# Exchanging real and imaginary spectrum rows with two strided transfers per unit, with a new order of work

## The chip, the cores and the metric

The kernel runs on one core of a Trainium2 chip. The metric is the device time of one execution in microseconds; the profiled span is the same execution from its first to its last instruction, about 2 us less. TensorE is PE, VectorE DVE, ScalarE ACT, GpSimd POOL, SyncE SP; SP issues nearly all transfers.

## The reference, cut to what matters

The result is a sum of three branches over the same normalised input: the input itself, a long convolution per channel, and a gated linear unit (GLU).

```python
xn = _layernorm(x, axis=-1)                       # x: [1, 2048, 512] bf16
# A: K[d,l] = Re sum_n C[d,n] exp(dt A[d,n] l) dB[d,n];  y = irfft(rfft(xn) * rfft(K)) + xn * Dskip
# B: h = sigmoid(xn @ w_gate) * (xn @ w_up);  h @ w_down          # F = 1792
return x + _A_ref(xn, ...) + _B_ref(xn, ...)
```

The convolution is a product of complex spectra. A complex product needs each real part beside the imaginary part of the same frequency, and the other way round. That exchange is what the change is about. The "up-projection" named below is the GLU's `xn @ w_up`.

## The kernel before

PE carries the GLU (672 of its matmuls of 512 columns) and a two-stage Fourier transform by matmul. Of the convolution's work the following parts matter here.

Nearly everything of the convolution lives in one tile of SBUF (the on-chip memory that all engines read), `big`, of 118,112 bytes per partition, cut by hand into regions that are reused: power tables `G` and `H`, input rows `xn`, later the exchange's buffers `xx`, kernel spectra `kb`, products `pp` and so on.

```python
big = const.tile([128, NBIG // 2], BF, name="big")
def at(off, shape, dt=BF):                         # a region of big
    v = big[:, off // 2:(off + n) // 2]
    ...
HOME = dict(xx=[OFF["xn"], OFF["xn"] + US, OFF["xn"] + 2 * US], ...)   # three buffers of 4 KB
```

There are 16 units: 8 pairs of frequency groups, for 2 halves of the channels. For each unit matmuls make the spectrum from a loaded input z, ACT evicts it (copies it out of PSUM, the memory that matmuls write) into `xx[:, 0]`, and transfers write it with real and imaginary rows exchanged into `xx[:, 1]`. A partition block of 64 rows holds 32 real rows and then 32 imaginary ones, so four transfers of 32 rows each do it. DVE then multiplies both copies by the kernel's spectrum, which matmuls make with a loaded constant matrix E. A unit's result v is stored to device memory and loaded again later.

```python
ex = pl.add("ACT", 0.91, fe, [mm], QP, rel=[sl])                       # eviction into xx[:, 0]
sws = [dma("SP", lambda xx=xx, b=b: xx()[32 * b:32 * b + 32, 1, :, :],
           lambda xx=xx, b=b: xx()[32 * (b ^ 1):32 * (b ^ 1) + 32, 0, :, :], deps=[ex], ...)(64 * KB)
       for b in range(4)]
...
pa_ = pl.add("DVE", 1.14, fpa, [ek] + sws, PKD, acq=[psl])             # pp = xx * kb, 128 x 2048
```

The kernel records operations and issues them in a fixed order, the list `ORDER`, found by a search. Each engine runs its instructions in that order. The waits between engines, on counters called semaphores, are not written by hand: they are derived when the program is built, from which instructions touch which bytes of a tile.

Of the kernel before, what the change touches and what calls it, by code (L numbers as in the profile page):

```python
# [59 lines left out]
MAGIC = 12582912.0  # L60
KB = 1024

def _th(s, b, k2):
    return 2 * np.pi * (s * b / 2048.0 + k2 * b / 32.0)

# [23 lines left out]
def _build_M2():  # L89
    M2 = np.zeros((NU, 128, 128))  # L90
    b = np.arange(32)[:, None]
    k2 = np.arange(32)[None, :]
    for g in range(NU):
        for par in range(2):
            s = 2 * g + par
            blk = slice(64 * par, 64 * par + 64)
            M = np.zeros((64, 64))
            if s >= 1:
                t = _th(s, b, k2)
                M[0:32, 0:32] = np.cos(t)  # L100
                M[32:64, 0:32] = np.sin(t)
                M[0:32, 32:64] = -np.sin(t)
                M[32:64, 32:64] = np.cos(t)
            else:
                t0 = 2 * np.pi * k2 * b / 32.0
                M[0:32, 0:16] = np.cos(t0)[:, 0:16]
                M[0:32, 32 + 1:32 + 16] = -np.sin(t0)[:, 1:16]
                M[0:32, 32 + 0] = (-1.0) ** b[:, 0]
                t64 = 2 * np.pi * (32 + 64 * (k2 - 16)) * b / 2048.0
                M[32:64, 16:32] = np.cos(t64)[:, 16:32]  # L110
                M[32:64, 32 + 16:32 + 32] = -np.sin(t64)[:, 16:32]
            M2[g, blk, blk] = M
    return M2

def _build_MAB():
    MA = np.zeros((NU, 128, 128))
    MB = np.zeros((NU, 128, 128))
    k2 = np.arange(32)[:, None]
    b = np.arange(32)[None, :]
    for g in range(NU):  # L120
        for par in range(2):
            s = 2 * g + par
            blk = slice(64 * par, 64 * par + 64)
            A = np.zeros((64, 64))
            B = np.zeros((64, 64))
# [10 lines left out]
            else:  # L136
# [9 lines left out]
                A[32 + 16:64, 32:64] = -2 * np.cos(t64)[16:32]  # L146
                B[16:32, 32:64] = -2 * np.sin(t64)[16:32]
                B[32 + 16:64, 32:64] = -2 * np.sin(t64)[16:32]
            MA[g, blk, blk] = A
            MB[g, blk, blk] = B  # L150
    return MA, MB

def _row(l):
# [22 lines left out]
def _consts():  # L176
# [27 lines left out]
    return dict(SR=f(sr), ident=f(np.eye(128)), S1=f(z1.reshape(128, 2, 128)), S2=f(z2.reshape(128, 2, 128)), M2=f(quads(M2)), SW=f(sw),  # L204
                MAB=f(np.stack([quads(MA, True), quads(MB, True)], axis=2)), E=f(_build_E(M2).reshape(128, NU // 2, 2, NKT, 128).transpose(1, 0, 2, 3, 4)))

UEV = (18, 19, 27, 28, 29, 30, 31, 32, 33, 34, 35, 36, 37, 38, 39, 40, 41, 44, 45, 52)
ON_ACT = (0, 2)
ORDER = [
    1, 0, 4, 37, 38, 28, 47, 39, 27, 40, 41, 2, 3, 48, 49, 5, 50, 12, 29, 51, 17, 52, 53, 42, 23, 24, 26, 10, 44, 30, 31,  # L210
    43, 32, 7, 6, 45, 46, 33, 34, 107, 35, 19, 25, 134, 36, 54, 644, 55, 645, 632, 633, 58, 15, 14, 106, 634, 646, 685, 686,
    131, 11, 59, 695, 121, 696, 675, 680, 105, 108, 109, 94, 93, 676, 8, 22, 9, 92, 681, 132, 655, 638, 639, 656, 95, 96,
    60, 56, 660, 640, 661, 665, 110, 97, 135, 18, 16, 13, 670, 666, 672, 682, 61, 671, 120, 673, 119, 62, 683, 98, 684, 118,
    100, 650, 662, 663, 651, 674, 136, 102, 101, 99, 133, 63, 140, 664, 700, 647, 57, 652, 701, 64, 648, 122, 141, 653, 649,
    123, 654, 20, 690, 691, 180, 146, 692, 693, 657, 66, 103, 104, 142, 694, 667, 658, 65, 67, 668, 659, 669, 227, 68, 147,
    69, 635, 687, 688, 636, 677, 689, 678, 124, 637, 70, 679, 641, 143, 697, 72, 127, 642, 71, 702, 73, 643, 137, 703, 698,
    138, 74, 699, 704, 75, 76, 736, 705, 111, 731, 112, 77, 181, 228, 182, 229, 78, 706, 79, 733, 732, 230, 183, 707, 231,
    81, 139, 148, 80, 114, 734, 82, 708, 738, 735, 155, 83, 737, 128, 739, 232, 184, 84, 185, 740, 186, 85, 713, 87, 187,
    156, 781, 115, 714, 86, 88, 149, 751, 715, 90, 144, 113, 157, 188, 145, 190, 198, 782, 752, 709, 199, 193, 150, 783,
    161, 721, 723, 724, 152, 191, 200, 784, 722, 202, 785, 201, 153, 203, 725, 116, 233, 761, 206, 741, 176, 766, 207, 192,  # L220
    194, 762, 742, 125, 195, 767, 154, 151, 208, 117, 726, 756, 763, 177, 727, 757, 158, 162, 178, 209, 204, 771, 758, 210,
    764, 765, 759, 773, 167, 772, 205, 21, 163, 126, 189, 774, 760, 753, 728, 211, 729, 89, 775, 754, 214, 168, 196, 159,
    212, 129, 169, 730, 213, 160, 755, 215, 743, 746, 170, 164, 216, 744, 747, 91, 217, 218, 745, 171, 197, 219, 165, 234,
    788, 748, 749, 786, 787, 371, 166, 716, 220, 221, 222, 750, 235, 776, 130, 172, 778, 173, 237, 240, 789, 245, 246, 790,
    768, 249, 223, 247, 777, 248, 174, 250, 253, 175, 847, 224, 241, 238, 239, 242, 244, 769, 225, 779, 770, 780, 791, 254,
    839, 792, 793, 255, 256, 432, 433, 257, 251, 817, 258, 259, 226, 402, 840, 260, 261, 794, 263, 403, 236, 717, 799, 372,
    243, 274, 818, 434, 252, 262, 264, 438, 404, 275, 265, 276, 266, 373, 374, 267, 269, 268, 277, 819, 278, 439, 408, 284,
    321, 279, 379, 406, 409, 280, 270, 292, 322, 293, 323, 837, 800, 296, 324, 820, 290, 286, 436, 378, 377, 294, 437, 295,
    297, 271, 801, 272, 287, 300, 273, 375, 298, 821, 291, 440, 289, 285, 405, 435, 301, 441, 838, 325, 407, 454, 376, 302,
    442, 841, 864, 443, 410, 303, 857, 380, 288, 865, 848, 411, 827, 444, 858, 412, 381, 828, 795, 304, 382, 305, 462, 469,  # L230
    802, 807, 867, 455, 445, 868, 463, 413, 306, 456, 464, 808, 308, 803, 283, 383, 307, 281, 447, 814, 812, 414, 384, 310,
    813, 385, 815, 311, 446, 309, 299, 387, 465, 862, 893, 863, 448, 844, 842, 449, 843, 467, 894, 312, 282, 816, 866, 394,
    466, 468, 424, 386, 451, 415, 452, 453, 470, 313, 450, 869, 859, 388, 326, 471, 472, 327, 389, 314, 860, 315, 473, 316,
    872, 331, 395, 339, 332, 392, 390, 416, 393, 391, 317, 417, 457, 873, 870, 396, 333, 861, 458, 340, 474, 822, 475, 341,
    823, 845, 871, 425, 829, 343, 477, 484, 830, 397, 344, 342, 418, 849, 419, 426, 559, 846, 831, 345, 854, 459, 850, 852,
    855, 422, 460, 347, 476, 421, 420, 398, 346, 874, 478, 552, 423, 853, 334, 479, 328, 851, 348, 856, 499, 349, 427, 399,
    834, 336, 337, 835, 875, 482, 876, 481, 483, 480, 428, 485, 900, 809, 486, 400, 553, 832, 350, 461, 554, 833, 810, 429,
    351, 487, 898, 811, 488, 824, 352, 430, 318, 401, 825, 507, 836, 489, 335, 353, 826, 330, 179, 354, 943, 355, 490, 899,
    357, 508, 555, 431, 492, 558, 509, 901, 338, 556, 557, 491, 529, 510, 329, 512, 358, 513, 877, 493, 356, 359, 494, 319,
    511, 360, 910, 361, 495, 497, 496, 320, 902, 362, 911, 363, 945, 364, 365, 953, 878, 498, 366, 622, 620, 618, 369, 367,  # L240
    560, 561, 562, 879, 946, 880, 563, 500, 530, 501, 502, 531, 514, 885, 597, 598, 503, 515, 604, 589, 522, 895, 886, 599,
    896, 897, 624, 504, 603, 516, 517, 505, 564, 903, 601, 602, 600, 565, 605, 523, 506, 524, 887, 518, 582, 519, 566, 616,
    606, 528, 526, 527, 525, 954, 904, 607, 520, 583, 908, 944, 909, 584, 608, 537, 925, 933, 913, 544, 574, 538, 934, 588,
    586, 609, 585, 532, 888, 539, 610, 926, 533, 923, 567, 914, 590, 545, 920, 587, 924, 591, 521, 542, 611, 630, 955, 927,
    568, 540, 543, 541, 918, 546, 569, 592, 956, 921, 919, 593, 626, 922, 534, 535, 594, 912, 957, 547, 905, 573, 595, 570,
    571, 548, 572, 575, 536, 906, 576, 577, 938, 940, 948, 549, 578, 596, 579, 939, 949, 941, 889, 370, 881, 942, 550, 958,
    915, 916, 580, 959, 612, 928, 917, 368, 551, 930, 581, 931, 929, 935, 628, 963, 950, 951, 613, 936, 627, 629, 617, 947,
    907, 932, 960, 937, 952, 614, 961, 619, 962, 964, 890, 623, 615, 891, 967, 965, 710, 625, 892, 711, 966, 631, 712, 621,
    968, 969, 804, 718, 805, 971, 719, 806, 970, 972, 882, 883, 796, 975, 720, 797, 884, 798, 973, 976, 978, 974, 979, 977,
    980, 981]  # L250

class _Op:
    __slots__ = ("alt", "tab", "eng", "cost", "fn", "prio", "acq", "rel", "dma", "left", "users", "ready", "start", "done", "seq", "mode")
# [57 lines left out]
def kernel(  # L311
# [567 lines left out]
    for p in range(NP):  # L879
        dsl = slice(DW * p, DW * p + DW)  # L880
        for u in range(NU // 2):
            gs = slice(2 * u, 2 * u + 2)
            QP = PK[p] + 0.01 * u
# [15 lines left out]
            def fe(sl=sl, xx=xx):  # L899
                S.activation(out=xx()[:, 0].rearrange("p h (g d) -> p g h d", g=2),  # L900
                             in_=two(sl).rearrange("p (g h d) -> p g h d", g=2, h=2), func=ACT.Identity)
            ex = pl.add("ACT", 0.91, fe, [mm], QP, rel=[sl])
            sws = [dma("SP", lambda xx=xx, b=b: xx()[32 * b:32 * b + 32, 1, :, :],
                       lambda xx=xx, b=b: xx()[32 * (b ^ 1):32 * (b ^ 1) + 32, 0, :, :], deps=[ex], prio=QP, pkt=2048, hv=0.5)(64 * KB)
                   for b in range(4)]
            le = dma("SP", es, cten["E"].ap()[u], deps=w_use[0], prio=QP - 0.5, acq=[esl], pkt=2560, hv=0.9)(320 * KB)
            sk = _Slot("s")

# [236 lines left out]
```

## Time and profile before

| | before |
|---|---|
| time, median of 3 (lowest to highest) | 240.98 us (240.19 to 241.13) |
| span of the profiled run | 238.5 us |
| busy PE / DVE / ACT | 227.5 / 187.5 / 181.6 us |
| mean granted PE clock | 0.998 |
| exchange transfers | 64 of 64 KB, 3.1 us from issue to landing (median) |
| DVE's waits for exchanges, in all | 6.8 us |

Busy PE is not PE at its peak, but here it says enough: outside the first and last few microseconds only some 6 us of the span find PE without a matmul. From 100 to 160 us DVE is full as well, and ACT 81 to 100% busy. The prediction below shows the lines.

### The profile page before, as it was taken

The numbers are of one execution on the slowest core, as the hardware profiler recorded it, in microseconds if no ns is written. First come the engines' busy times: TensorE is split into PE (matmuls) and PEld (weight loads), VectorE is DVE, ScalarE is ACT, GpSimd is POOL, SyncE is SP. The second block draws the span as 40 slices with busy tenths as digits, with TensorE's granted clock in tenths as the row PEclk, the third lists the DMA queues.
The fourth block names the chain that finished last, engine by engine and source line by source line (L and its number), as shares of the span: only waits on it lengthen the run. The fifth ranks groups of instructions, "written<-read, shape, count | busy, mean of one in ns | idle before, by whom it ended". The sixth has DMA issues, their size and how long they took to land.

```text
span 238.5 us, 5382 instructions
## 1 busy us (share of the span) xinstructions
PE 227.5 (95%) x2074; PEld 113.8 (48%) x2074; DVE 187.5 (79%) x397; ACT 181.6 (76%) x294; POOL 18.4 (8%) x42
## 2 busy tenths in 40 slices
PE   7989999999999999999999999999999989799993
PEld 2455444444444454366545744436655455344441
DVE  3999899999999999999999999991334516672562
ACT  5999999999999997778998999976467878520000
POOL 1205210002000020100010500000000030000000
PEclk9999999999999999999999999999999999999999
DMA  5999795204366597474677386675677789579253
GB/s 155 223 355 328 229 353 133 91 0 88 132 168 219 162 179 206 85 214 88 204 162 215 91 237 183 185 214 128 187 198 197 222 168 275 157 198 290 98 193 104
DMA packets 50859, 43.60 MB, mean 183 GB/s; under 512 B 12561, under 2 KB 44050, under 8 KB 50834
## 3 DMA queue, kind: packets, MB, share of 16 engines
q1 hardware_dynamic: 48738, 40.58, 60.0%
q0 software_dynamic: 864, 1.57, 4.4%
q10 hardware_dynamic: 1232, 1.11, 1.4%
q8 instruction: 16, 0.26, 0.4%
q14 instruction: 9, 0.07, 0.1%
HBM read 24.64 MB, written 12.06 MB: 154 GB/s over the span
## 4 chain that ended last, share of the span: by engine, by line
PE 42%; ACT 24%; DMA 14%; DVE 7%; SPq 6%; issue 5%; ACTq 0%; DVEq 0%
PE bank L1074 15%; DMA big<-big 9%; PE bank L1026 7%; ACT hT_sb L1035 5%; SPq L417 4%; PE pair L913 4%; PE bank L1041 4%; ACT big L666 3%; PE pair L820 3%; ACT big L697 3%; DMA wg_sb<-in_B_w_gate_dram 3%; ACT big L672 3%; DVE big L919 2%; DMA big<-v_scr 2%; ACT big L558 2%
## 5 line engine op out<-in xcount | busy, mean ns | idle before, releaser
L1026 PE MATMUL bank<-xnT,wg_sb 128*128 128x512 bf16 (+1 forms) x236 | 55.4, 369 | 1.6 <-DMA wg_sb<-in_B_w_gate_dram 0.9
L1041 PE MATMUL bank<-xnT,wu_sb 128*128 128x512 bf16 x224 | 54.5, 380 | 0.1
L1074 PE MATMUL bank<-wd_sb,hT_sb 128*128 128x512 bf16 x224 | 51.0, 380 | 0.4 <-ACT glu_sb L1104 0.3
L1035 ACT ACTIVATE hT_sb<-bank 128x512 bf16<-128x512 f32 x56 | 33.2, 614 | 3.9 <-PE bank L1026 3.8
L1026 PEld LDWEIGHTS <-wg_sb 128*128 128x128 bf16 x236 | 21.5, 97 | 26.6 <-issue 5.1
L1074 PEld LDWEIGHTS <-hT_sb 128*128 128x128 bf16 x224 | 21.4, 98 | 26.3 <-issue 1.6
L1041 PEld LDWEIGHTS <-wu_sb 128*128 128x128 bf16 x224 | 21.2, 98 | 25.3 <-issue 2.0
L919 DVE TENSOR_TENSOR big<-big 128x2048 bf16<-128x2048 bf16 x16 | 19.4, 1219 | 16.1 <-DMA big<-big 6.8
L1056 DVE TENSOR_TENSOR hT_sb<-hT_sb,bank 128x512 bf16<-128x512 bf16 x36 | 24.0, 683 | 9.5 <-PE bank L1041 6.2
L731 DVE TENSOR_TENSOR big<-big 128x1024 bf16<-128x1024 bf16 (+4 forms) x40 | 25.9, 648 | 0.6 <-ACT big L772 0.3
L732 DVE TENSOR_TENSOR big<-big 128x1024 bf16<-128x1024 bf16 (+4 forms) x40 | 25.8, 646 | 0.0
L913 PE MATMUL pair<-big 128*128 128x256 bf16 x160 | 19.8, 273 | 0.4 <-DVE big L855 0.3
L900 ACT ACTIVATE big<-pair 128x1024 bf16<-128x1024 f32 x16 | 16.3, 1028 | 4.8 <-PE pair L895 4.7
L915 ACT ACTIVATE big<-pair 128x1024 bf16<-128x1024 f32 x16 | 16.5, 1035 | 3.9 <-PE pair L913 3.2
L940 ACT ACTIVATE big<-pair 128x1024 bf16<-128x1024 f32 x16 | 16.3, 1032 | 3.5 <-PE pair L936 1.7
L913 PEld LDWEIGHTS <-big 128*128 128x128 bf16 x160 | 15.5, 98 | 5.5 <-issue 1.1
L736 DVE TENSOR_TENSOR big<-big 128x512 bf16<-128x512 bf16 (+4 forms) x40 | 16.9, 424 | 0.2
L697 ACT ACTIVATE big<-pair 128x1024 bf16<-128x1024 f32 x16 | 16.9, 1058 | 0.0
L737 DVE TENSOR_TENSOR big<-big 128x512 bf16<-128x512 bf16 (+4 forms) x40 | 16.9, 422 | 0.0
L788 ACT ACTIVATE sq_sb<-big 128x256 bf16<-128x256 bf16 (+2 forms) x20 | 13.0, 657 | 2.4 <-DVE big L737 1.8
L936 PE MATMUL pair<-big 64*64 64x512 bf16 (+1 forms) x256 | 13.0, 327 | 1.4 <-DVE big L919 1.4
L772 ACT ACTIVATE big<-big 128x256 bf16<-128x256 bf16 x32 | 13.2, 459 | 1.0 <-PE pair L820 1.0
(106 smaller groups left out, 275.9 us busy)
## 6 DMA issues: line engine op xcount, KB each, us to landing
big<-c_E SPq DMA_DIRECT2D x16, 320.0 KB, 4.4
z_scr<-big SPq DMA_DIRECT2D x16, 256.0 KB, 2.6
big<-z_scr SPq DMA_DIRECT2D x16, 256.0 KB, 3.8
big<-big SPq DMA_DIRECT2D x64, 64.0 KB, 3.1
v_scr<-big SPq DMA_DIRECT2D x16, 256.0 KB, 3.5
big<-v_scr SPq DMA_DIRECT2D x12, 256.0 KB, 5.0
big<-in_A_u_dram SPq DMA_DIRECT2D x4, 512.0 KB, 5.2
wu_sb<-in_B_w_up_dram SPq DMA_DIRECT2D x2, 896.0 KB, 8.6
```

Source lines behind the costliest of these rows:

```text
L697: ev = pl.add("ACT", 0.90, lambda sl=sl, zs=zs: S.activation(out=zs().rearrange("p j d -> p (j d)"), in_=two(sl), func=ACT.Identity), [fx_ ...
L731: V.tensor_tensor(out=wide(outp), in0=wide(lo), in1=mre, op=ALU.mult)
L732: V.tensor_tensor(out=wide(tb()), in0=wide(lo), in1=mim, op=ALU.mult)
L736: V.tensor_tensor(out=outp[:, :, :, 0, :], in0=outp[:, :, :, 0, :], in1=tb()[:, :, :, 1, :], op=opr)
L737: V.tensor_tensor(out=outp[:, :, :, 1, :], in0=outp[:, :, :, 1, :], in1=tb()[:, :, :, 0, :], op=opi)
L913: T.matmul(two(sk)[:, o:o + DW], es()[:, g, kt, :], kT[p][:, kt, :], start=kt in (0, NKT - 1), stop=kt >= NKT - 2)
L919: V.tensor_tensor(out=pp().rearrange("p q h m -> p (q h) m"), in0=xx().rearrange("p q h m -> p (q h) m"), in1=kb()[:, 0:2 * DW].unsqueeze( ...
L1026: T.matmul(bank(sl)[:, c0:c1], w[:, kt, k * 128:(k + 1) * 128], xnT[:, grp, kt, c0:c1], start=(kt == 0), stop=(kt == KT - 1))
L1035: S.activation(out=hT_sb[:, hs.idx, k % 2, :], in_=bank(sl), func=ACT.Sigmoid)
L1041: T.matmul(bank(sl), wu_sb[:, kt, k * 128:(k + 1) * 128], xnT[:, grp, kt, :], start=(kt == 0), stop=(kt == KT - 1))
L1056: V.tensor_tensor(out=h(), in0=h(), in1=us_sb[:, us.idx, :] if on else bank(sl), op=ALU.mult)
L1074: T.matmul(bank(po), hT_sb[:, hts[k // 2].idx, k % 2, jj * 128:(jj + 1) * 128], wd_sb[:, k, :], start=(k == 0), stop=k == FT - 1, **kw)
```

## The change

The intent: put real and imaginary rows on alternate partitions, so that two transfers with a partition step of two do the exchange. 32 issues on SP go; the bytes are the same. The matrices' rows and columns are permuted to match, and the order was searched anew.

```diff
+PAIR = np.arange(64).reshape(2, 32).T.reshape(64)
-            M2[g, blk, blk] = M
+            M2[g, blk, blk] = M[:, PAIR]
-            MA[g, blk, blk] = A
-            MB[g, blk, blk] = B
+            MA[g, blk, blk] = A[PAIR]
+            MB[g, blk, blk] = B[PAIR]
-UEV = (18, 19, 27, 28, ...)        # 20 up-projections evicted by ACT
-ON_ACT = (0, 2)
-ORDER = [1, 0, 4, 37, 38, ...]     # 982 operations
+UEV = (19, 21, 23, 25, ...)        # 22
+ON_ACT = (1, 3)
+ORDER = [1, 0, 37, 27, 28, ...]    # 950 operations
...
-            sws = [dma("SP", lambda xx=xx, b=b: xx()[32 * b:32 * b + 32, 1, :, :],
-                       lambda xx=xx, b=b: xx()[32 * (b ^ 1):32 * (b ^ 1) + 32, 0, :, :], deps=[ex], prio=QP, pkt=2048, hv=0.5)(64 * KB)
-                   for b in range(4)]
+            sws = [dma("SP", lambda xx=xx, b=b: xx()[b:128:2, 1, :, :], lambda xx=xx, b=b: xx()[1 - b:128:2, 0, :, :], deps=[ex], prio=QP,
+                       pkt=2048, hv=0.5)(128 * KB) for b in range(2)]
```

## The prediction

> **What bounds the kernel now.** I read the page's busy shares first, then the slices, the stretches of 10 us, the chain of work that ended last, the groups, and last the transfers, both the page's medians and the answer for the one line that issues nearly all of them.
>
> ```profile
> PE 227.5 (95%) x2074; PEld 113.8 (48%) x2074; DVE 187.5 (79%) x397; ACT 181.6 (76%) x294; POOL 18.4 (8%) x42
> PE   7989999999999999999999999999999989799993
> DVE  3999899999999999999999999991334516672562
> PEclk9999999999999999999999999999999999999999
> PE 42%; ACT 24%; DMA 14%; DVE 7%; SPq 6%; issue 5%; ACTq 0%; DVEq 0%
> ```
>
> PE is never long without work: 238.5 us of span against 227.5 busy, and of the 11 us idle 1.4 lie ahead of the first matmul and 3.4 after the last. That leaves about 6 us of gaps that a better order could close. Its clock is full throughout. DVE is full until slice 27 (about 161 us) and then a third to two thirds busy.
>
> ```profile
> 100.00:110.00 10.00, 10.00 (x225) 5.92 (x224) 9.90 (x33) 8.47 (x16) 0.00 (x0) 1.00 0.71 175
> 140.00:150.00 10.00, 9.90 (x81) 4.45 (x78) 10.00 (x18) 9.99 (x16) 0.00 (x0) 1.00 0.70 197
> 180.00:190.00 10.00, 10.00 (x72) 4.58 (x72) 4.52 (x6) 7.85 (x12) 0.00 (x0) 1.00 0.77 216
> ```
>
> Columns: stretch, its length, busy PE, PEld, DVE, ACT, POOL, clock, DMA share, GB/s. From 100 to 160 us PE, DVE and ACT are all full together: table building (power tables, DVE and ACT), spectrum products and GLU run side by side. Whatever stops two of the three here lengthens the stage.
>
> ```profile
> 121.35 1.02 ACT big L900
> 122.37 0.50 ACT hT_sb L1035
> 122.97 0.58 SPq L417
> 123.60 0.57 SPq L417
> 124.22 0.51 SPq L417
> 124.77 4.83 DMA big<-big
> ```
>
> This is the changed place, in the chain (start, length): the eviction L900 writes a unit's spectrum, SP issues exchange transfers at about 0.6 us each, they land, and DVE multiplies (L919). The transfers' sizes and latencies:
>
> ```profile
> big<-big SPq DMA_DIRECT2D x64, 64.0 KB, 3.1
> big<-c_E SPq DMA_DIRECT2D x16, 320.0 KB, 4.4
> big<-z_scr SPq DMA_DIRECT2D x16, 256.0 KB, 3.8
> big<-v_scr SPq DMA_DIRECT2D x12, 256.0 KB, 5.0
> DMA to landing us min/median/max: 1.9/3.3/6.5
> L919 DVE TENSOR_TENSOR big<-big 128x2048 bf16<-128x2048 bf16 x16 | 19.4, 1219 | 16.1 <-DMA big<-big 6.8
> ```
>
> The fifth line is for the issuing line from 96 to 162 us. DVE waits only 6.8 us in all for exchanges: latency is mostly hidden, because other work on the same large buffer goes on during it.
>
> **What the Trainium skill says.** "SBUF — State Buffer", section "An operand's partitions come from dim 0 alone": a compute engine's operand must step exactly one row per partition. So only the transfers can take every second partition; the products and matmuls stay as they are, and the matrices' rows are permuted instead. The trace agrees in that every compute operand here is a consecutive block. "DMA: Bandwidth & Descriptors", "Anatomy of one DMA": a fixed part of about 2 us, mostly completion, dominates a small transfer (its fit is for another issue path), and semaphore waits are done by the issuing sequencer before dispatch. The trace agrees: 64 KB takes 1.9 us at best, so 128 KB should take little more; and a wait on SP stops every transfer behind it. "TensorE: Matmul & The Clock Gate", part 1: after an idle window of about 3.4 us the PE clock halves until it has been busy for as long. The kernel before never shows it.
>
> **The change, part by part.**
>
> Intended gain. Per unit two issues go: 16 x 2 x 0.58 = 18.6 us of SP, and about 1.2 us between eviction and last landing. As L919 waits 6.8 us for exchanges in total, and PE is 95% busy, that is worth at most 2 to 3 us of the end. Bytes are the same. Two more up-projections are evicted by ACT (22, not 20): 2 x 0.63 us on ACT, 2 x (0.68 - 0.42) off DVE. Nothing. The reordered PE sequence switches between full-array and tiled matmuls about as often as before. Alone, I would call all this -1 us.
>
> What the listing of the built programs shows. I compared the instructions with the semaphores they wait for, and traced each wait to the instruction that satisfies it. Before, 16 DVE and 13 ACT instructions wait on an exchange, all of them the product L919 or the reuse of its buffer. In the changed program:
>
> ```
> L736 TensorTensor big_95<-big_95 128x64x4x2 [waits DMAHW2_49,DVE_49]
> L788 Activation sq_sb_73<-big_95 128x768 [waits DMAHW5_49,DMAHW2_49,DVE_49]
> L820 Ldweights big_95 [waits DVE_49,Activation_49,DMAHW2_49]
> L417 DMACopy big_95<-big_95 64x1024 [waits DMAHW4,3,5,1,6,0,7 _49,DVE_49,Activation_49]   (names joined here)
> ```
>
> The first three are table work that touches no byte of the exchange; they wait for it all the same. The fourth, an exchange, waits for seven transfers, the last DVE and the last ACT instruction. All these live in one SBUF tile, `big`; a transfer with a partition step of two seems to be taken as touching all of it. So every exchange is a barrier over `big`: everything issued before it there must end, and everything after it waits until it lands, on DVE, ACT, PE, POOL and SP alike. 120 waits of SP's transfers have no overlap in bytes behind them (2 before). Only GLU matmuls, sigmoids and GLU products that stand at the head of their queue go on.
>
> Count of barriers: 32 exchanges, of which 22 stand as adjacent pairs with no DVE work between: 10 single + 11 paired = 21. With little else in flight I take 2.5 us for a single (between the best 1.9 and the median 3.1), one issue of 0.58 more for a pair: 10 x 2.5 + 11 x 3.1 = 59 us.
>
> Work between them: going through the changed order and giving each instruction the duration of its kind in the trace before (pitch where they follow closely: 0.07 + 0.00052 per column for DVE products, 0.91 for a 1024-column eviction), the larger of DVE and ACT in the 20 stretches between barriers is 6.9, 3.7, 5.8, 0, 5.4, 6.8, 6.8, 1.2, 1.8, 8.2, 6.3, 2.6, 3.8, 3.9, 6.9, 1.4, 10.2, 1.1, 1.8, 2.3: together 87 us. PE's own work there is about 95 us, which is why the kernel before crosses this part in 100 us.
>
> Serial transfers: in six places the next exchange waits for a load that itself waited for the last one, longer than the engines' work: a spectrum load and an E load (0.6 + 0.6 + 4.4) between two exchanges of one unit, less PE's share, 4.5 us; E loads 4; z loads 1.5 and 1.8; v loads 5 and 3.3. Together 20 us.
>
> Sum. First exchange: 100.6 us before; 2.6 us more PE work precedes it now: 103. From first to last exchange: 87 + 59 + 20 = 166. After the last: 38 us before (200.7 to 238.5); now one barrier is counted already, 37. Total 306. GLU work done inside barriers takes off perhaps 8 us. Chains from ACT to DVE and back inside the short stretches, which ran under other work before, add perhaps 10. Half-clock spells add more: I expect some six PE gaps beyond 3.4 us, each followed by a window at half speed, 6 x 1.7 = 10 us at most, say 6. 306 - 8 + 10 + 6 = 314.
>
> **The rivals.** (1) The waits are in the program but long satisfied when reached, as with most waits before; then the time is 238 to 241. For it: PE carries enough GLU work, and L919 hardly waited before. Against: the barrier takes in the *latest* DVE and ACT instruction, and the next one waits for a landing; with DVE full from 100 to 160 us that cannot be early. (2) DVE and ACT stall, but PE, which has 95 us of work for the stage, fills the barriers with GLU matmuls, and only part of 59 us shows: 260 to 280. For it: GLU matmuls don't touch `big`. Against: PE's queue is in order and a tiled or spectrum matmul stands every 1 to 3 us; PE then waits with the rest. (3) The exchange takes longer in strided form: +1 us on each barrier, 330 to 340. Against: rows stay 2 KB, and 64 rows spread as well as 32.
>
> **Range and chances.** The lower end takes 2.2 us barriers, serial loads half hidden and PE filling well: 314 - 8 - 10 - 12 = 284. The upper takes the loaded median latency, 21 x 0.6 = 13 more, and longer chains: 350. Faster only if the waits did not act.
>
> **What would show it.** Right: DVE and ACT at four to six tenths from 100 us on; "DMA big<-big" at the head of the list of waits for DVE, ACT and PE, table lines (L731, L736, L772, L788, L820) among those waiting; the chain alternating between exchange and one short piece of work, its DMA share well over 30%; 32 exchanges of 128 KB with a landing of 2 to 3 us; PEclk falling below 9 in places; the first 100 us and last 37 us as before. Wrong: DVE full again to 160 us would refute the barrier; PE 90% busy would mean rival 2; a landing over 4 us, rival 3.

## The result, and the profile after

| | before | changed |
|---|---|---|
| time, median | 241.06 us (4 runs) | 316.48 us (4 runs, 315.02 to 317.64) |
| ratio of times | | 1.3136, 95% interval 1.3069 to 1.3204 |
| span | 238.5 us | 313.7 us |
| mean granted PE clock | 0.998 | 0.907 |

Ratios here are the mean time of one kernel's fast runs over that of the other's fast runs of the same rounds, so they are not quite the ratio of the medians.

The page of the changed kernel: busy shares, three rows of the slices (one slice is now 7.8 us), and the shares of the chain of work that ended last, by engine and by line.

```profile
PE 245.4 (78%) x2046; PEld 121.8 (39%) x2074; DVE 187.0 (60%) x397; ACT 183.8 (59%) x296; POOL 18.3 (6%) x42
...
PE   8989999999999296649781838585897495378995
...
DVE  4989999989999465724872266461053132127164
...
PEclk9999999999999689767798798779799899697999
...
DMA 33%; PE 23%; DVE 21%; ACT 13%; SPq 5%; issue 4%; DVEq 0%; ACTq 0%
DMA big<-big 15%; PE bank L1073 6%; DMA big<-z_scr 6%; DMA big<-c_E 4%; DVE hT_sb L1055 3%; PE bank L1025 3%; DVE big L732 3%; SPq L417 3%; DVE big L731 3%; PE pair L912 3%; PE pair L820 3%; PE bank L1040 3%; DVE big L736 2%; SPq L445 2%; DMA v_scr<-big 2%
```

The same last line of the page before:

```profile
PE bank L1074 15%; DMA big<-big 9%; PE bank L1026 7%; ACT hT_sb L1035 5%; SPq L417 4%; PE pair L913 4%; PE bank L1041 4%; ACT big L666 3%; PE pair L820 3%; ACT big L697 3%; DMA wg_sb<-in_B_w_gate_dram 3%; ACT big L672 3%; DVE big L919 2%; DMA big<-v_scr 2%; ACT big L558 2%
```

The work of DVE and ACT is what it was (187.0 against 187.5 us, 183.8 against 181.6), but it is spread over 75 us more. Up to slice 13 the rows look as before. From the 14th on, about 102 us, all three engines fall together, which is what a common wait looks like and a full engine doesn't. Transfers held 14% of the chain before (33 us); now they hold 33% (103 us), and exchanges alone 15%, which is 47 us (before 9%, 21 us).

The list of waits of the changed kernel (who waited for what: us in total, times, longest) names the waiters. POOL's lines at its head are left out, since POOL isn't on the chain.

```profile
...
ACT big L900 <- DMA big<-big: 24.9, 5, 9.2
...
DVE big L736 <- DMA big<-big: 18.7, 5, 4.8
DVE big L922 <- DMA big<-big: 17.8, 6, 5.8
DVE big L731 <- DMA big<-big: 17.1, 3, 7.8
...
ACT sq_sb L788 <- DMA big<-big: 13.3, 3, 8.4
...
PE pair L842 <- DMA big<-big: 7.5, 2, 4.8
```

L731, L736 and L788 build the power tables, L842 selects from the convolution kernel's values: none of them reads or writes a byte of `xx`. Before, L919 was the only DVE line that waited for an exchange at all. One stretch of the chain shows how a barrier grows long (start us, length us, what).

```profile
131.17 0.61 DVE big L922
131.83 1.91 DMA big<-big
133.75 0.38 SPq L417
134.19 3.23 DMA big<-c_E
137.48 1.96 DMA big<-big
139.55 0.84 ACT sq_sb L788
```

DVE ends a product at 131.8. An exchange can then be issued, and lands after 1.91 us. Only then can a load of E (which shares no byte with it) be issued; it takes 3.23 us; the next exchange, which waits for that load, takes 1.96 us more. From 131.8 to 139.5 us neither DVE nor ACT starts anything that touches `big`. Among the stretches of 10 us up to 170 us this is the one in which DVE and ACT do least (columns as in the prediction: stretch, length, busy PE, PEld, DVE, ACT, POOL, clock, DMA share, GB/s).

```profile
90.00:100.00 10.00, 9.95 (x109) 4.62 (x108) 9.96 (x25) 8.62 (x18) 1.02 (x2) 1.00 0.69 185
...
130.00:140.00 10.00, 6.27 (x33) 2.53 (x33) 2.23 (x5) 1.60 (x3) 0.00 (x0) 0.67 0.24 85
```

The transfers of the changed kernel, size and median from issue to landing:

```profile
big<-c_E SPq DMA_DIRECT2D x16, 320.0 KB, 3.6
...
big<-big SPq DMA_DIRECT2D x32, 128.0 KB, 2.0
```

The strided exchange itself is quick: twice the bytes of one before in 2.0 us instead of 3.1, since so little else is in flight.

### The profile page after: what moved, and what is told of

The parts are those of the page before. It is cut to its first block, busy times and chain, and to the rows that moved or that the text cites. A ratio compares the mean times of both kernels' runs of the same rounds, so it can differ in the third digit from the quotient of the medians.

```text
span 313.7 us, 5317 instructions
## 1 busy us (share of the span) xinstructions
PE 245.4 (78%) x2046; PEld 121.8 (39%) x2074; DVE 187.0 (60%) x397; ACT 183.8 (59%) x296; POOL 18.3 (6%) x42
## 4 chain that ended last, share of the span: by engine, by line
DMA 33%; PE 23%; DVE 21%; ACT 13%; SPq 5%; issue 4%; DVEq 0%; ACTq 0%
DMA big<-big 15%; PE bank L1073 6%; DMA big<-z_scr 6%; DMA big<-c_E 4%; DVE hT_sb L1055 3%; PE bank L1025 3%; DVE big L732 3%; SPq L417 3%; DVE big L731 3%; PE pair L912 3%; PE pair L820 3%; PE bank L1040 3%; DVE big L736 2%; SPq L445 2%; DMA v_scr<-big 2%
## 5 line engine op out<-in xcount | busy, mean ns | idle before, releaser
L1025 PE MATMUL bank<-xnT,wg_sb 128*128 128x512 bf16 (+1 forms) x226 | 59.1, 392 | 7.0 <-ACT hT_sb L1034 5.1
L1040 PE MATMUL bank<-xnT,wu_sb 128*128 128x512 bf16 x214 | 58.6, 404 | 2.9 <-issue 1.3
L731 DVE TENSOR_TENSOR big<-big 128x1024 bf16<-128x1024 bf16 (+4 forms) x40 | 25.9, 647 | 17.6 <-DMA big<-big 17.1
L1025 PEld LDWEIGHTS <-wg_sb 128*128 128x128 bf16 x236 | 23.5, 103 | 32.9 <-issue 11.0
L912 PE MATMUL pair<-big 128*128 128x256 bf16 x160 | 24.2, 309 | 13.7 <-DMA big<-c_E 6.9
L900 ACT ACTIVATE big<-pair 128x1024 bf16<-128x1024 f32 x16 | 16.4, 1024 | 30.5 <-DMA big<-big 24.9
L935 PE MATMUL pair<-big 64*64 64x512 bf16 (+1 forms) x256 | 16.7, 388 | 15.6 <-ACT big L900 9.5
L736 DVE TENSOR_TENSOR big<-big 128x512 bf16<-128x512 bf16 (+4 forms) x40 | 16.9, 423 | 18.8 <-DMA big<-big 18.7
L912 PEld LDWEIGHTS <-big 128*128 128x128 bf16 x160 | 17.3, 110 | 21.7 <-issue 9.6
L788 ACT ACTIVATE sq_sb<-big 128x256 bf16<-128x256 bf16 (+2 forms) x20 | 12.9, 647 | 20.5 <-DMA big<-big 13.3
L914 ACT ACTIVATE big<-pair 128x1024 bf16<-128x1024 f32 x16 | 16.3, 1023 | 11.0 <-PE pair L912 10.0
L922 DVE TENSOR_TENSOR big<-big 128x1024 bf16<-128x1024 bf16 x16 | 11.0, 687 | 17.8 <-DMA big<-big 17.8
L939 ACT ACTIVATE big<-pair 128x1024 bf16<-128x1024 f32 x16 | 16.4, 1025 | 5.3 <-DMA v_scr<-big 4.1
L935 PEld LDWEIGHTS <-big 64*64 64x64 bf16 x256 | 8.4, 120 | 26.0 <-issue 22.6
```

The lines of the kernel that those rows point to most:

```text
L731: V.tensor_tensor(out=wide(outp), in0=wide(lo), in1=mre, op=ALU.mult)
L736: V.tensor_tensor(out=outp[:, :, :, 0, :], in0=outp[:, :, :, 0, :], in1=tb()[:, :, :, 1, :], op=opr)
L900: S.activation(out=xx()[:, 0].rearrange("p h (g d) -> p g h d", g=2), in_=two(sl).rearrange("p (g h d) -> p g h d", g=2, h=2), func=ACT.Id ...
L912: T.matmul(two(sk)[:, o:o + DW], es()[:, g, kt, :], kT[p][:, kt, :], start=kt in (0, NKT - 1), stop=kt >= NKT - 2)
L935: T.matmul(two(sv)[o:o + 64, DW * (2 * g + y):2 * DW * (g + 1)], mab[b:b + 64, 2 * u + g, q, :], pq()[b:b + 64, q, ch] if y else pp()[b:b ...
L1025: T.matmul(bank(sl)[:, c0:c1], w[:, kt, k * 128:(k + 1) * 128], xnT[:, grp, kt, c0:c1], start=(kt == 0), stop=(kt == KT - 1))
```

## The experiments

The theory: strided transfers bring waits into the built program that nothing in the data asks for, and these make each exchange a barrier. Rival A: the new order is bad. Rival B: a strided transfer is slow on the chip. All kernels below gave a correct result.

### 1. The new order without strided transfers

Old row layout, and two contiguous transfers in each of the new order's exchange operations.

```diff
-            M2[g, blk, blk] = M[:, PAIR]      # likewise MA, MB
+            M2[g, blk, blk] = M
-            sws = [dma(... xx()[b:128:2, 1, :, :] ... xx()[1 - b:128:2, 0, :, :] ...) for b in range(2)]
+            for b in (c, c + 2):              # c = 0, 1: the operation
+                Y.dma_start(out=xx()[32 * b:32 * b + 32, 1, :, :], in_=xx()[32 * (b ^ 1):32 * (b ^ 1) + 32, 0, :, :])
```

> The new order of work, with the old row layout and four contiguous 64 KB transfers per unit (two per exchange operation of the order). Theory of barriers (waits that the strided transfers bring into the program stop DVE, ACT and PE): all of the loss goes, 235 to 242 us, the clock back at 0.99 or more. Rival A, the new order itself is bad: it stays above 290 us. Rival B, a strided transfer is slow on the chip: also 235 to 242, so this run does not tell B from the barriers.

Measured: 238.57 us, ratio 0.994 (0.988 to 1.000), clock 1.0. The whole loss is gone. Rival A falls.

### 2. Strided transfers in the old order

The kernel before with the new layout, and the two strided transfers where the first two of four stood.

```diff
-            sws = [dma("SP", ... xx()[32 * b:32 * b + 32, 1, :, :] ...)(64 * KB) for b in range(4)]
+            sws = [dma("SP", ... xx()[b:128:2, 1, :, :] ...)(128 * KB) for b in range(2)]
+            sws += [pl.add("SP", 0.0, lambda: None, sws[1:2], QP) for b in range(2)]    # empty, keeps the numbering
```

> The old order of work with the new row layout and two strided transfers per unit, issued where the first two of four stood. Barriers: as bad as the changed kernel or worse, 295 to 345 us, since the old order was not made for them either. Rival A: near 241 us. Rival B: 290 us or more.

Measured: 316.98 us, ratio 1.318, clock 0.897: the same loss in another order. So the loss doesn't depend on which of the two orders is used.

### 3. The change with its buffer cut up

Buffers of their own for `xx` would have taken 12 KB more per partition (219.5 KB asked for, 207.9 there). So the one tile was cut into six at the same addresses. Rows of `xn` and the exchange's buffers lie in four of them, one for each 4 KB; layout, order and transfers are those of the change.

```diff
-    big = const.tile([128, NBIG // 2], BF, name="big")
+    CUTS = [0, XN0, XN0 + 4 * KB, XN0 + 8 * KB, XN0 + 12 * KB, XN1, NBIG]      # 68096 and 84480
+    SEG = [const.tile([128, (b - a) // 2], BF, name="seg" + c) for a, b, c in zip(CUTS, CUTS[1:], "abcdef")]
...
-        v = big[:, off // 2:(off + n) // 2]
+        v = SEG[k][:, (off - CUTS[k]) // 2:(off + n - CUTS[k]) // 2]           # k: the segment of off
```

> The changed kernel with the one large buffer cut into six tiles at the same addresses, so that the exchange's buffers are three tiles of their own; strided transfers, layout and order unchanged. In the built program only the product and the eviction then wait for an exchange. Barriers: 235 to 242 us, exchange landing about 2.5 to 3.5 us at 128 KB under load. Rival B: still above 290 us, or landings well over 4 us. Rival A: above 290 us.

Measured: 235.12 us, ratio 0.978 (0.976 to 0.981), clock 1.0. In the built program only the product (16 times) and the eviction (13) still wait for an exchange among the engines' instructions. Rival B falls: these are the same strided transfers. The expected landing of 2.5 to 3.5 us was too short for two of the three buffers, though. From this kernel's page and its transfers:

```profile
PE 225.3 (97%) x2074; PEld 113.9 (49%) x2074; DVE 185.5 (79%) x397; ACT 181.3 (78%) x296; POOL 18.3 (8%) x42
...
PE 59%; DMA 13%; DVE 11%; ACT 9%; SPq 4%; issue 2%; DVEq 0%; ACTq 0%
...
segb<-segb SPq DMA_DIRECT2D x12, 128.0 KB, 4.4
segc<-segc SPq DMA_DIRECT2D x10, 128.0 KB, 3.7
segd<-segd SPq DMA_DIRECT2D x10, 128.0 KB, 2.6
```

`segb`, `segc` and `segd` are the three exchange buffers. Among other traffic an exchange takes 2.6 to 4.4 us, longer than the 2.0 of the slow kernel, and yet only one wait of DVE for it, of 2.5 us, is left in the list. A median of 4.4 us would by itself have passed for the sign of rival B. But in the repeat of this run (experiment 9) the three medians are 3.5, 3.8 and 3.1 us, and contiguous transfers of half the size take 3.3, 3.6 and 3.0 us in the same cut order (experiment 8). So strided transfers are not slow here.

```profile
DVE sege L930 <- DMA segb<-segb: 2.5, 1, 2.5
```

### 4 and 5. Half of the units strided

Strided transfers in units 0 to 3 of each half of the channels, contiguous ones in units 4 to 7, and the reverse.

```diff
-            M2[g, blk, blk] = M[:, PAIR]
+            M2[g, blk, blk] = M[:, PAIR] if g < 8 else M        # reverse: g >= 8
+                    if u < 4:                                   # reverse: u >= 4
+                        Y.dma_start(out=xx()[c:128:2, 1, :, :], in_=xx()[1 - c:128:2, 0, :, :])
+                        return
+                    for b in (c, c + 2): ...                    # contiguous, as in experiment 1
```

> The changed kernel with strided transfers in the first four of eight units of each half only, the other eight units with the old layout and four contiguous transfers. Barriers: about half of the 75 us, 265 to 290 us. If the cost came from the first few barriers alone, or from any one of them, it would be near 241 or near 316.

> The changed kernel with strided transfers in the last four of eight units of each half. The first four alone cost 54 us of 75. If the costs of barriers add up: 262 us. If each half costs much the same and the two share waits when together: 280 to 296.

Measured: 294.99 us (ratio 1.2266) and 265.72 us (1.1043). The first missed its expected range by 5 us: the cost is not even over the units. The two together, 22.7% and 10.4%, give 33.1% against 31.4% for all units strided. So the costs nearly add up, as barriers in different places would; nothing that only the first or the last of them does explains the loss. Why the earlier units cost twice as much wasn't tested. Part of it can be read in the two traces: SP issues the strided transfers of the earlier units at 13 separate places, those of the later ones, mostly pairs, at 9.

### 6 to 9. What the cut, the order and the two transfers are worth

The cut tile was applied to the kernel before, to the kernel of experiment 2 and to that of experiment 1, with no other edit, and the cut changed kernel was run again.

> Control: the kernel before with the buffer cut into six tiles at the same addresses, its own order, layout and four transfers. If cutting the tile has no effect of its own (the kernel before has hardly a wait without shared bytes): 240 to 242 us. If the cut itself brought the gain of the cut changed kernel, about 236.

> Cut tiles, the old order of work, two strided transfers per unit. Barriers: freed of them the two transfers cost nothing, 238 to 241 us, that is 0 to 3 us better than the kernel before. Rival B (strided transfers slow): above 245.

> Cut tiles, the new order, four contiguous transfers. With the earlier run of the new order uncut at 238.6 us: 237.5 to 239.5. Against the cut changed kernel at 235.1 this gives what two transfers in place of four are worth in the new order, about 3 us.

> The cut changed kernel once more, on the chip of the other cut kernels if it falls so, to settle whether it is over 2% faster than the kernel before and to complete the table of order by transfers: 234.5 to 236 us, ratio 0.975 to 0.981, some 3 us below the cut new order with four transfers (238.31).

| cut tile | four contiguous transfers | two strided transfers |
|---|---|---|
| old order | 240.79 us, ratio 0.9999 (0.9977 to 1.0021) | 238.23 us, 0.9907 (0.9884 to 0.9929) |
| new order | 238.31 us, 0.9902 (0.9879 to 0.9926) | 236.08 us, 0.9802 (0.9779 to 0.9826); first run 235.12 us, 0.9784 |

Each ratio is against the kernel before in the same rounds. The cut does nothing by itself: 240.79 us. With it in place, the two transfers save 2.6 us in the old order and 2.2 in the new (3.2 by the first run), and the order saves 2.5 with four transfers and 2.2 with two. The cut changed kernel ran on other chips than the other three; by the ratios, which compare within a chip, the four figures are 2.2, 2.4 (2.8), 2.3 and 2.5 us. The repeat came out 0.1 us above its expected range of times, and 2.2 us below the four transfers where some 3 were expected. So both parts of the change do what they were meant to, and the cut changed kernel beats the kernel before by about 2%. Whether that is more or less than 2% isn't settled: both intervals hold that value.

### 10 and 11. Keeping PE's clock up

The changed kernel with three, and then six, matmuls of no use ahead of each unit's first-stage and E matmuls. They stand before the instruction that waits, and read only weights and inputs that are there. But they write the PSUM bank of the unit's own matmuls, so they need it free: in the trace of the first kernel those ahead of the E matmuls waited 5.7 us for it themselves.

```diff
             def fm(sl=sl, u=u, zx=zx):
+                for _ in range(3):                # or 6; likewise in fk
+                    T.matmul(two(sl)[:, 0:512], wg_sb[:, 0, 0:128], xnT[:, 0, 0, :], start=True, stop=True)
```

> The changed kernel with three matmuls of no use (128x512, on weights already there) ahead of each unit's first-stage matmuls and of each unit's E matmuls: 96 in all, 21 us of extra PE work at full clock, standing where PE waits anyway. If half-clock spells cost about 6 us of the end, as predicted, and the extra work is mostly hidden: granted clock 0.93 to 0.96, 308 to 318 us. If low clock costs nothing on the path: the clock rises and the time is 316 to 330.

> The same with six each, 192 matmuls, 41 us of extra PE work. Granted clock above 0.95. With a clock term of 6 us and work mostly hidden 308 to 325 us; if PE's queue is then in the way of the next unit, more than 330.

Measured: 317.01 us (ratio 1.3138) at a clock of 0.933, and 327.29 us (1.3589) at 0.936. With three the clock rose from 0.907 and the time stayed; with six it rose no further and time was lost. The first lies in both of its expected ranges and so decides nothing; the second missed its clock (above 0.95) and fell between its two ranges. This doesn't settle what the low clock costs: the gain from a faster clock and the cost of the extra matmuls, 26 us busy with three each, may have met. It only says that this remedy isn't worth having.

### Where the waits come from: programs built, not run

To see what the derivation of waits does, I built small programs with one tile, a strided exchange of 64 rows, and a DVE instruction on columns far from it, and read the waits in them. Where the DVE operand is an unbroken run of columns, no wait comes. Where it has gaps (a slice of a four-level view), a wait came if the transfer is 512 or 1024 columns wide, and none at 256 or fewer:

```
TensorScalarPtr big<-big 128x64                          exchange of 1024 columns, unbroken operand
TensorScalarPtr big<-big 128x4x8 [waits DMAHW1_49]       exchange of 1024 columns, operand with gaps
TensorScalarPtr big<-big 128x4x8                         exchange of 256 columns, operand with gaps
```

Not every operand with gaps brings it. Programs of the same kind had the wait with a step of 164 columns, which is that of table `H`, and none with steps of 16, 64 or 256 columns, at any width; contiguous transfers of 64 rows never had it. So it is an overlap test that is exact only in part, and says "overlap" in the rest. What decides between the two wasn't found. In this kernel the tables' operands have gaps nearly everywhere.

## Why the prediction was right, point by point

- **The time.** 314 us was predicted and 316.48 measured, but the closeness is in part luck, as the next points show. The sum was built on spans, and the span is 313.7; the 2 us between span and time were left out.
- **The step that carries it,** that every exchange would act as a barrier for the engines and transfers on `big`, is shown: by the table lines that now wait for exchanges, by the loss in both orders with strided transfers, and by its absence when the same transfers lie in tiles of their own. Its wording was too broad. The prediction had a transfer with a partition step of two taken as touching the whole tile; the small programs show that it depends on its width and on the other operand.
- **The stages.** The first exchange was put at 103 us and is issued at 106.1: the chain shows it behind a load of E that ends at 105.4, where the prediction saw only 2.6 us more of PE's work. With the tile cut it is issued at 100.7. From there to the last landing, 281.4 us, are 175.3 us; the prediction's terms (166 - 8 + 10 + 6) give 174. What follows took 32.3 us; it was given 37, by a wrong reading: in the trace before, the last exchange is issued at 201.0 us and lands at 204.9, so 33.6 us followed it, and the prediction's 200.7 is in no view. The three errors, 3.1, 1.3 and -4.7 us, cancel.
- **Terms inside the middle stage** were less good than their sum. Barriers were given 59 us, SP's issues in them included; of the chain between first issue and last landing exchanges hold 46 us and SP's issues of all transfers 9, a landing being 2.0 us and not the 2.5 assumed. Serial loads of z, E and v were given 20 us; they hold 28, and stores of v 7 more. Work of the engines was given 87 - 8 + 10 = 89 us; PE, ACT and DVE hold 78. The errors are opposite.
- **The clock term** of 6 us: the granted clock did fall, to 0.67 in some stretches. Six long PE gaps were expected, and the timeline has eight, of 3.4 to 8.5 us. PE was busy 17.9 us longer with the same matmuls. How much of that lay on the path stays open after experiments 10 and 11.
- **The intended gain** was put at 2 to 3 us at most for the transfers, which is what 2.2 to 3.2 us confirm. The step that failed is the other one: "Alone, I would call all this -1 us", with nothing for the new order. Freed of the barriers the change is worth 4.8 to 5.7 us, of which the order brings 2.2 to 2.5. I had compared the two orders by their switches between matmul forms, and that says little.
- **The rivals.** (1), waits long satisfied, was wrong: 24.9 us of waiting on one line alone. (2), PE filling the barriers, was wrong in the main: from 100 to 282 us PE is busy for 123 of 182 us. (3), slow strided transfers, was wrong: 2.0 us.
- **The signs** came true in the main. DVE and ACT were at four to six tenths only until 200 us (55% and 52%); from 200 to 282 us they were at 28% and 43%. For PE the longest wait listed was for an eviction (9.5 us, L900), not for an exchange (7.5 us, L842).

## What to carry to other kernels

Before a transfer or an operand with an unusual pattern goes into a shared tile, read in the built program what it waits for and who waits for it: a wait between two instructions without a common byte is a loss that no duration in the old profile shows. Cutting a hand-managed buffer into tiles along the lines of its regions costs nothing (240.79 against 240.72 us here) and keeps a cautious overlap test from joining what is separate. In a trace such waits look like several engines falling idle together, with transfers at the head of the chain while little is moved.

## What the Trainium skill lacked or had wrong

- No page says that waits derived for a tile may join accesses without a common byte. "SBUF — State Buffer", section "An operand's partitions come from dim 0 alone", tells which partition steps are legal for engines, not what a strided transfer does to its neighbours in a tile: 241.06 us became 316.48, and 235.12 with the tile cut.
- "DMA: Bandwidth & Descriptors", "Anatomy of one DMA", gives about 2 us of fixed cost for another issue path. The runs agree for SP's transfers with little else in flight (128 KB in 2.0 us), and show what it lacks, the latency of a transfer within SBUF among other traffic: medians of 2.6 to 4.4 us for the same transfer in the cut kernel.
- "TensorE: Matmul & The Clock Gate", part 1, on the clock falling after an idle window: the runs agree (0.998 to 0.907, 0.67 in some stretches of 10 us, with eight PE gaps of 3.4 to 8.5 us). It doesn't say how to tell whether a low clock matters where PE waits anyway. Filling the waits with 96 matmuls brought the clock to 0.933 and the time not at all (ratio 1.3138 against 1.3136).
